# Decode attention over 64 heads: V of pair 30 in two halves, 64 stationary tokens in the last pair, and unused matmuls in the gaps of TensorE between its last parts

## The chip, the cores and the metric

The kernel runs on one core of a Trainium2 chip. The metric is device time in microseconds (us) of one execution, without the profiler's help; the profile of one execution is read beside it. Its span, from the first instruction to the last, is some 2 us shorter than the measured time (671.3 us for the run of 673.07 us that was profiled before). "Full" and "half" clock are the granted TensorE clock of 1.0 and 0.5 in the trace.

## The reference, cut to what matters

Two independent attention blocks, A and B, are computed for one query token each, with 32 heads, 8192 cached tokens and 128 channels per head; the two output rows of 512 are put side by side.

```python
q = (x @ wq)                                   # 1 x 32 heads x 128
scores = einsum("bhqd,bhkd->bhqk", q, k_cache) * 128 ** -0.5
p = softmax(scores)
o = einsum("bhqk,bhkd->bhqd", p, v_cache)
y = o.reshape(1, 32 * 128) @ wo                # ... A and B, concatenated
```

K and V of 64 heads in bf16 are 268 MB, read once. The kernel treats heads in pairs: 32 pairs, 0 to 31, each with one K and one V of 4 MB.

## The kernel before

K and V pass through a ring of five slots of 4 MB in SBUF. The order of the last transfers is K30, K31, wo (output weights of B, without its last two heads), V29, V30, V31 in three parts, the two heads of wo. For each pair, DVE multiplies K by q (`plan_M`, L422), TensorE folds the 128 products of a token to 8 with identity matmuls of 512 columns (`plan_fold`, L177 and L181, two halves a pair), DVE sums those (`plan_R`), a short exchange finds the maximum, ACT does exp, and TensorE multiplies with V:

```python
def plan_PV(j, t0=0, t1=TP, end=TP):                  # "wide": V moves, 512 columns a matmul,
    ...                                               # four matmuls side by side in the array
    for i in range(t0, t1, TB):                       # TB = 4 tokens x 128 partitions
        g = (i // TB) % CG
        m = e.matmul(ot_ps[...][32 * g:32 * g + 2 * TB, :], p2[:, ..., i:i + TB, :], t[:, i:i + TB, :], ...)
    ...                                               # then ACT copies ot_ps to o8
def plan_ot(j, last=True):                            # the fp32 "turn": 8 matmuls on o8, L552
    W('PE', c_cp, cp_val[j])                          # waits for that copy
    ...
def plan_PVturned(j, t0, t1):                         # "stationary tokens": V is the weight, 2 columns move
    for i in range(t0, t1):
        m = e.matmul(st_ps[1][:, 0:2], t[:, i, :], p2[:, ..., i, :], ...)
```

TensorE works in program order. Its last stage, for pairs 29 to 31, reads as follows (calls of other engines cut). `plan_y` multiplies 24 and then 4 finished heads with wo, 4 matmuls a head with one moving column each: the "light" stretch. `plan_ysq` is an output block of 8 matmuls for one pair.

```python
plan_PV(j - 2)                  # V29, 32 wide matmuls, L526: "the start of the last stage" below
plan_tr(j); plan_ot(j - 2); ...
for b in early: plan_y(LA, *b[:2])                    # 96 light matmuls, L652
plan_w_ready(j - 2); plan_sum(j); ...; plan_y(...)    # 16 more, L652
plan_PV(j - 1); plan_ot(j - 1); plan_o(j - 1)         # V30
LW = LAST_PARTS[NLW - 1][1]                           # parts (0, 64), (64, 96), (96, 128); NLW = 2
for i, (t0, t1) in enumerate(LAST_PARTS):             # V31
    W('PE', *part_of[i])                              # wait for this part's transfer
    if t1 <= LW:
        plan_PV(j, t0, t1, LW)
    else:
        if t0 == LW:
            plan_ot(j, False)                         # the turn stands BEHIND the wait
        plan_PVturned(j, t0, t1)                      # last 32 tokens
    if i == 0:
        plan_ysq(0)
plan_o(j)
plan_ysq(1)                                           # last output block, L689; DVE casts, SP stores
```

Of the kernel before, what the change touches and what calls it, by code (L numbers as in the profile page):

```python
# [39 lines left out]
def bass_concat_heads__mha_block_cached__gqa_block_cached__decode_kernel(  # L40
# [23 lines left out]
    Dh = ks[0].shape[3]  # L64
# [12 lines left out]
    NPR = NA * PPA  # L77
# [24 lines left out]
    with ExitStack() as st:  # L102
# [56 lines left out]
        def W(eng, ctr, val):  # L159
            if val is None or val <= 0:  # L160
                return
            if waited.get((eng, ctr.name), 0) >= val:
                return
            waited[(eng, ctr.name)] = val
            prog[eng].append((ctr, val))

        def OP(eng, fn):
            prog[eng].append(fn)
# [104 lines left out]
        land_of = {}  # L273
# [24 lines left out]
        assert order[-1] == ('v', NPR - 1)  # L298
        for name in order:
            item(name)  # L300
        LAST_PARTS = [(0, 64), (64, 96), (96, 128)]
        NLW = 2
        part_of = {}
        wo_early = wo_plan[LA][:-1]
        issued = [0]

        def dma(dst, src, ctr):
            v = ctr.bump(16)
            OP('SP', lambda e: e.dma_start(dst, src).then_inc(ctr.sem, 16))
            return v  # L310

        def issue(n):
            kind, idx = queue[n]
            s = n % NS
            if n >= NS:
                assert free_of[n - NS] is not None, (queue[n], queue[n - NS])
                for ctr, val in free_of[n - NS]:
                    W('SP', ctr, val)
            if kind in ('k', 'v'):
                a, jj = divmod(idx, PPA)  # L320
                t = (ks if kind == 'k' else vs)[a][0, 2 * jj:2 * jj + 2]
                src = t.rearrange("h (p t) d -> (h p) (t d)", t=TP)
                if (kind, idx) == ('v', NPR - 1):
                    for i, (t0, t1) in enumerate(LAST_PARTS):
                        part_of[i] = (s_part[i], dma(ring[:, s, t0 * Dh:t1 * Dh],
                                                     src[:, t0 * Dh:t1 * Dh], s_part[i]))
                else:
                    land_of[(kind, idx)] = dma(ring[:, s, :], src, s_slot[s])
            elif kind == 'wq':
                land_of[(kind, idx)] = dma(  # L330
                    ring[:, s, 0:NC_ * H * Dh],
                    wqs[idx].rearrange("(p c) n -> p (c n)", p=P), s_slot[s])
            else:
                for blk in wo_early if idx == LA else wo_plan[idx]:
                    land_of[('wo', idx, 0)] = (s_slot[s], load_wo(idx, s, blk, s_slot[s]))
            if (kind, idx) == ('v', NPR - 1):
                h0, n_, pm = wo_plan[LA][-1]
                for i in range(n_):
                    ctr = s_part[len(LAST_PARTS) + i]
                    land_of[('wo', LA, 1 + i)] = (ctr, load_wo(  # L340
                        LA, slot_of[('wo', LA)], (h0 + i, 1, pm), ctr))

# [71 lines left out]
        def kv(name):  # L414
            return ring[:, slot_of[name], :].rearrange("p (t d) -> p t d", d=Dh)
# [96 lines left out]

        def plan_PV(j, t0=0, t1=TP, end=TP):

            if ('v', j) in land_of:
                landed('PE', ('v', j))
            W('PE', c_e, e_val[j])
            W('PE', c_init, INIT)
            if t0 == 0 and j >= 1:
                W('PE', c_cp, cp_val[j - 1])  # L520
            t = kv(('v', j))

            def op(e):
                for i in range(t0, t1, TB):
                    g = (i // TB) % CG
                    m = e.matmul(ot_ps[j % NS % 2][32 * g:32 * g + 2 * TB, :],  # L526
                                 p2[:, j % NS, i:i + TB, :].rearrange("p t h -> p (t h)"),
                                 t[:, i:i + TB, :].rearrange("p t d -> p (t d)"),
                                 start=(i < TB * CG), stop=(i >= end - TB * CG))
                if t1 == end:  # L530
                    m.then_inc(c_pv.sem, 1)
            OP('PE', op)
            if t1 < end:
                return
            v = pv_val[j] = c_pv.bump()
            if end == TP:
                release(('v', j), (c_pv, v))
            W('ACT', c_pv, v)
            if j >= 1:
                W('ACT', c_ot, ot_val[j - 1])  # L540
            cp_val[j] = INC('ACT', c_cp, lambda e: e.copy(o8[:, j % NS % 2, :], ot_ps[j % NS % 2][:]))  # L541
# [16 lines left out]

        def plan_PVturned(j, t0, t1):
            t = kv(('v', j))  # L560

            def op(e):
                for i in range(t0, t1):
                    m = e.matmul(st_ps[1][:, 0:2], t[:, i, :], p2[:, j % NS, i, :],
                                 start=False, stop=(i == TP - 1), skip_group_check=True)
                if t1 == TP:
                    m.then_inc(c_ot.sem, 1)
            OP('PE', op)
            if t1 == TP:
                ot_val[j] = c_ot.bump()  # L570
                release(('v', j), (c_ot, ot_val[j]))
# [59 lines left out]
        def plan_y(a, h0, n):  # L631

            W('PE', *land_of[('wo', a, 0)])
            W('PE', c_w, w_val[(a, h0)])
            first = h0 == 0
            if first and a:
                W('PE', c_ye, a)
            last = not any(pm and b > h0 for b, _, pm in wo_plan[a])
            v = c_y.bump() if last else None

            def row(e):
                for i in range(n):
                    m = e.matmul(y_ps[0:1, :], w_bf[:, a, h0 + i:h0 + i + 1], wo_of(a)[:, h0 + i, :],  # L643
                                 start=(first and i == 0), stop=(last and i == n - 1),
                                 skip_group_check=True)
                if last:
                    m.then_inc(c_y.sem, 1)

            def cols(e):
                for i in range(n):  # L650
                    for b in range(NB):
                        m = e.matmul(y_ps[:, b:b + 1], wo_of(a)[:, h0 + i, b * P:(b + 1) * P],  # L652
                                     w_bf[:, a, h0 + i:h0 + i + 1],
                                     start=(first and i == 0 and b == 0),
                                     stop=(last and i == n - 1), skip_group_check=True)
                if last:
                    m.then_inc(c_y.sem, 1)
            OP('PE', cols if a == LA else row)
            if not last:
                return  # L660
            W('ACT', c_y, v)
            if a != LA:
                release(('wo', a), (c_y, v))
                ve = INC('ACT', c_ye, lambda e: e.copy(y_row[:], y_ps[0:1, :]))
                W('ACT', c_ye, ve)
                s_out.bump(16)
                OP('ACT', lambda e: e.dma_start(
                    out[0, 0:1, a * NOUT:(a + 1) * NOUT], y_row[:]).then_inc(s_out.sem, 16))
                return
            ve = INC('ACT', c_ye, lambda e: e.copy(y_bulk[:], y_ps[:, 0:NB]))  # L670
            W('PE', c_ye, ve)
            if qw_free[0]:
                W('PE', *qw_free[0])
            OP('PE', lambda e: e.matmul(qw_ps[0:NB, 0:P], y_bulk[:], ident_f[:],
                                        start=True, stop=False, skip_group_check=True))

        def plan_ysq(i):
# [18 lines left out]
            if last:  # L696
# [6 lines left out]
                    out[0, 0, LA * NOUT:(LA + 1) * NOUT].rearrange("(b m) -> b m", b=NB),  # L703
                    y_sb[:]).then_inc(s_out.sem, 16))



        for a in range(NA):
# [6 lines left out]
        def plan_w_ready(jo):  # L715

            for h0, n, pm in perm_l:
                if h0 not in w_done and LA * PPA + (h0 + n) // 2 - 1 <= jo:
                    w_done.add(h0)
                    plan_w(LA, h0, n)  # L720

        marks = []
        for j in range(NPR):
            marks.append({eng: len(ops) for eng, ops in prog.items()})
            c = j >= 1
# [50 lines left out]
        plan_o(j - 2)  # L776
        for b in early:
            plan_y(LA, *b[:2])
        plan_w_ready(j - 2)
        plan_sum(j)  # L780
        plan_ri(j)
        assert len(w_done) == len(perm_l) and len(direct_l) == 2
        for b in perm_l[len(early):]:
            plan_y(LA, *b[:2])
        plan_PV(j - 1)
        plan_ot(j - 1)
        plan_o(j - 1)
        LW = LAST_PARTS[NLW - 1][1]
        for i, (t0, t1) in enumerate(LAST_PARTS):
            W('PE', *part_of[i])  # L790
            if t1 <= LW:
                plan_PV(j, t0, t1, LW)
            else:
                if t0 == LW:
                    plan_ot(j, False)
                plan_PVturned(j, t0, t1)
            if i == 0:
                plan_ysq(0)
        plan_o(j)
        plan_ysq(1)  # L800
        assert issued[0] == len(queue)
# [82 lines left out]
```

## Time and profile before

| | before |
|---|---|
| time | 672.9 us, median of 3 (672.36 to 673.01); profiled run 673.07 us, span 671.3 us |
| traffic | 285 MB, mean 425 GB/s |
| last part of V31 landed | 665.58 us |
| from there to the last instruction's end | 5.7 us |
| last stage, from V29's matmuls (647.67) to the end of the cast (669.41) | 21.7 us, of which 2.1 us wait for V |

Two rows of the page, busy share in 40 equal slices, in tenths; the first is the granted clock of TensorE:

```profile
PEclk9998876779877767888876789877767888798787
DMA  9999999999999999999999999999999999999995
```

The DMA engines are busy until the last transfers run out (share 1.00 from 659.49 to 662.90 us, 0.46 in the 3.41 us after that). The chain of waits (start, duration in us, what) therefore ends in one long transfer and what follows it:

```profile
...
635.32 30.26 DMA ring<-in_B_v_cache_dram
665.58 0.04 issue
665.62 1.26 PE stps L552 x8
666.89 0.87 PE stps L564 x32
...
667.85 0.19 DVE sq L585
...
668.08 1.03 PE qwps L689 x8
...
669.13 0.28 DVE y_sb L699
```

The eight fp32 turns L552 do not need the last part of V; they wait for it by program order alone. The next fence is the timeline of TensorE in the last stage, with one line of ACT (start, duration, engine, line, count, and in brackets the idle time before it and what ended it):

```profile
...
647.67 1.90 PE L526 MATMUL otps<-ring,p 128*8 128x512 bf16 x32
...
655.99 3.80 PE L526 MATMUL otps<-ring,p 128*8 128x512 bf16 x29
660.47 1.05 PE L552 MATMUL stps<-sel,o 128*128 128x2 f32 x8 [0.68 <-ACT o L541]
661.45 1.04 PE L526 MATMUL otps<-ring,p 128*8 128x512 bf16 x16
662.31 0.61 PE L689 MATMUL qwps<-ring,sq 128*4 128x128 bf16 x8
663.13 0.60 PE L526 MATMUL otps<-ring,p 128*8 128x512 bf16 x8 [0.20 <-DMA ring<-in_B_v_cache_dram]
663.78 0.58 ACT L541 COPY o<-otps 128x512 f32<-128x512 f32 x1 [3.37 <-PE otps L526]
...
665.62 1.26 PE L552 MATMUL stps<-sel,o 128*128 128x2 f32 x8 [1.89 <-DMA ring<-in_B_v_cache_dram]
```

The bracketed 0.20 and 1.89 us are 2.1 us of waits for V. The turn also needs ACT's copy of the wide matmuls' sums, which ended at 664.36 us; where no transfer was late, a turn with nothing in between began 0.68 to 0.79 us after the wide matmuls before it. V29's 32 wide matmuls take 1.90 us and V30's take twice as long, because the clock differs. The windows between the clock's steps show it (stretch, length, busy us of each engine with counts, granted clock, DMA share, GB/s):

```profile
649.25:652.66 3.41, 2.92 (x63) 2.46 (x56) 0.44 (x2) 1.53 (x5) 0.00 (x0) 1.00 1.03 442
652.66:656.07 3.41, 3.11 (x86) 2.81 (x87) 0.52 (x3) 0.35 (x3) 0.00 (x0) 0.50 0.99 413
656.07:659.49 3.42, 3.42 (x33) 1.22 (x25) 0.00 (x0) 0.00 (x0) 0.00 (x0) 0.50 0.93 393
659.49:662.90 3.41, 2.73 (x37) 1.77 (x32) 0.18 (x1) 0.58 (x1) 0.00 (x0) 1.00 1.00 411
```

The clock fell after the first of these, though TensorE is shown busy for 2.92 of 3.41 us: from 650.26 us on, 2.4 us, that is matmuls with one or two moving columns (the turn, two small ones, and 1.1 us of the light stretch). It rose after the third window, which V30's matmuls filled.

"Activity" of a window, below, is my count from the trace: moving columns over the granted rate (about 2.4 columns a ns at full clock, as 15 folds of 512 columns took 3.24 us), a quarter for the wide matmuls that run four side by side, four times for fp32 (at half clock one of 128 columns, L674, took 0.42 us), over 3.41 us. These four windows have 0.08, 0.35, 0.92 and 0.38.

### The profile page before, as it was taken

Reading aid. Unit: us, or ns where it says so; the run is one execution under the profiler, and the core shown is the slowest. Engines: PE = TensorE matmul, PEld = TensorE weight load, DVE = VectorE, ACT = ScalarE, POOL = GpSimd, SP = SyncE. Lnnn points to the kernel's source line nnn. Section 1 sums busy time; section 2 is a strip of 40 time slices with the busy share of each in tenths; the row PEclk is TensorE's granted clock in tenths of the full one; section 3 lists DMA queues with packets and bytes.
Section 4 is the critical chain, followed back from the end, with each engine's and each line's share of the span. In section 5 each row is a group of like instructions: output and inputs, shape, how many; then the busy total and the mean of one; then the engine's idle time right before and its main releaser. Section 6 shows DMA issues by size and latency. Waiting matters only on the chain.

```text
span 671.3 us, 6004 instructions
## 1 busy us (share of the span) xinstructions
PE 439.0 (65%) x2782; PEld 102.8 (15%) x1822; DVE 387.5 (58%) x517; ACT 61.9 (9%) x203; POOL 2.4 (0%) x16
## 2 busy tenths in 40 slices
PE   2765775655677666567765655777566567757696
PEld 0200110101111010111111101111011111121134
DVE  5194566665555666555566665556666555555840
ACT  0101101001111001111100011110101111101010
POOL 1000000000000000000000000000000000000000
PEclk9998876779877767888876789877767888798787
DMA  9999999999999999999999999999999999999995
GB/s 375 437 437 433 430 421 431 437 436 432 421 428 437 437 433 430 420 435 437 433 435 428 424 435 437 433 433 422 430 437 435 433 428 424 433 436 429 426 422 240
DMA packets 10953, 285.38 MB, mean 425 GB/s; under 512 B 1211, under 2 KB 1726, under 8 KB 1854
## 3 DMA queue, kind: packets, MB, share of 16 engines
q1 hardware_dynamic: 10936, 285.22, 99.0%
q8 instruction: 8, 0.13, 0.1%
q14 instruction: 3, 0.02, 0.0%
q10 hardware_dynamic: 6, 0.00, 0.0%
HBM read 285.21 MB, written 0.00 MB: 425 GB/s over the span
## 4 chain that ended last, share of the span: by engine, by line
DMA 62%; PE 24%; DVE 11%; issue 2%; SPq 0%; DVEq 0%
DMA ring<-in_B_k_cache_dram 30%; DMA ring<-in_A_k_cache_dram 28%; PE fold L181 15%; DVE ring L422 8%; DMA ring<-in_B_v_cache_dram 5%; PE otps L526 3%; PE fold L177 2%; PE stps L552 1%; DVE s_sb L448 1%; PE yps L643 1%; DVE m L459 1%; PE stps L477 1%; DVE wt L614 0%; DVE w_bf L623 0%; DVE rinv L502 0%
## 5 line engine op out<-in xcount | busy, mean ns | idle before, releaser
L422 DVE TENSOR_TENSOR ring<-ring,qbc 128x2048 bf16<-128x2048 bf16 x256 | 298.4, 1216 | 166.5 <-DMA ring<-in_A_k_cache_dram 93.7
L181 PE MATMUL fold<-ring,ident 128*128 128x512 bf16 x960 | 276.3, 452 | 0.0
L467 PE MATMUL stps<-ident_f,m 128*2 128x128 f32 x32 | 11.1, 348 | 141.7 <-DVE rinv L502 140.2
L177 PE MATMUL fold<-ring,ident 128*128 128x512 bf16 x64 | 31.4, 491 | 64.6 <-DVE ring L422 64.6
L526 PE MATMUL otps<-ring,p 128*8 128x512 bf16 x1016 | 62.7, 387 | 0.2 <-DMA ring<-in_B_v_cache_dram 0.2
L552 PEld LDWEIGHTS stps<-sel,o 128*128 128x128 f32 x256 | 33.6, 192 | 157.3 <-issue 152.1
L448 DVE TENSOR_REDUCE s_sb<-fold 128x64 f32<-128x512 f32 x64 | 44.0, 688 | 3.2 <-PE fold L181 2.6
L483 ACT COPY nb<-stps 128x1 f32<-128x1 f32 x32 | 5.1, 159 | 419.2 <-PE stps L477 419.2
L585 DVE TENSOR_TENSOR ot<-stps,rinv 128x2 f32 (+1 forms) x30 | 4.8, 160 | 62.5 <-PE stps L552 62.5
L552 PE MATMUL stps<-sel,o 128*128 128x2 f32 x256 | 30.9, 243 | 3.1 <-DMA ring<-in_B_v_cache_dram 1.9
L541 ACT COPY o<-otps 128x512 f32<-128x512 f32 x32 | 18.7, 585 | 135.7 <-PE otps L526 135.7
L489 ACT ACTIVATE p<-s_sb,nb 64x128 bf16<-64x128 f32 x64 | 28.0, 437 | 3.8
L496 PEld LDWEIGHTS stps<-rowsum,ones_f 128*128 128x128 f32 x64 | 12.3, 194 | 98.7 <-issue 97.9
L467 PEld LDWEIGHTS stps<-ident_f,m 128*2 128x2 f32 x32 | 2.6, 81 | 158.8 <-DVE m L459 132.0
L526 PEld LDWEIGHTS otps<-ring,p 128*8 128x8 bf16 x1016 | 22.5, 87 | 24.3 <-issue 1.6
L387 PE MATMUL qwps<-ring,xsel 128*128 128x512 bf16 x64 | 18.6, 443 | 9.3 <-ACT qbc L394 4.8
L459 DVE TENSOR_REDUCE m<-s_sb 64x1 f32<-64x128 f32 x64 | 17.9, 280 | 2.1
L177 PEld LDWEIGHTS fold<-ring,ident 128*128 128x128 bf16 x64 | 6.4, 99 | 78.0 <-issue 59.6
L614 DVE TENSOR_TENSOR wt<-qwps,hmask 128x512 f32<-128x512 f32 (+3 forms) x5 | 2.2, 441 | 21.4 <-PE qwps L607 21.3
L477 PE MATMUL stps<-m,sel 2*128 2x1 f32 x64 | 12.1, 256 | 0.0
L489 ACT ACTIVATION_READ_ACCUMULATOR p<-s_sb,nb 64x1 f32 x64 | 11.6, 181 | 0.0
L477 PEld LDWEIGHTS stps<-m,sel 2*128 2x128 f32 x64 | 9.4, 182 | 10.5 <-issue 10.0
(49 smaller groups left out, 80.1 us busy)
## 6 DMA issues: line engine op xcount, KB each, us to landing
ring<-in_A_k_cache_dram SPq DMA_DIRECT2D x16, 4096.0 KB, 39.4
ring<-in_A_v_cache_dram SPq DMA_DIRECT2D x16, 4096.0 KB, 31.9
ring<-in_B_k_cache_dram SPq DMA_DIRECT2D x16, 4096.0 KB, 39.4
ring<-in_B_v_cache_dram SPq DMA_DIRECT2D x15, 4096.0 KB, 32.0
ring<-in_A_wq_dram SPq DMA_DIRECT2D x1, 4096.0 KB, 12.1
ring<-in_B_wq_dram SPq DMA_DIRECT2D x1, 4096.0 KB, 21.4
ring<-in_A_wo_dram SPq DMA_DIRECT2D x1, 4096.0 KB, 39.9
ring<-in_B_wo_dram SPq DMA_DIRECT2D x1, 2048.0 KB, 34.6
```

The source lines that it names most:

```text
L177: return e.matmul(out, lhsT, rhs, start=start, stop=stop)
L181: return e.add_instruction(mybir.InstMatmult(name=nc.get_next_instruction_name(), engine=e.engine, ins=[e.lower_ap(rhs), e.lower_ap(lhsT)] ...
L387: m = e.matmul(qw_ps[:, :].rearrange("p (j d) -> p j d", d=Dh), xsel[:, a, c, par, :], wq[:, c, 4 * g:4 * g + 4, par, :], start=(i == 0), ...
L422: m_val[(j, i)] = INC('DVE', c_m, lambda e: e.tensor_tensor(t, t, qbc[:, at(j, 1), :].broadcast_to([P, CH, Dh]), ALU.mult))
L448: r_val[(j, h)] = INC('DVE', c_r, lambda e: e.tensor_reduce(s_sb[:, j % NS, h * HT:(h + 1) * HT], fold_ps[h][:, :].rearrange("p (t e) -> p ...
L459: m1_val[j] = INC('DVE', c_m1, lambda e, h=h, q0=q0, q1=q1: e.tensor_reduce(m1[q0:q1, j % NS, h:h + 1], s_sb[q0:q1, j % NS, :], AX.X, ALU. ...
L467: tr_val[j] = INC('PE', c_tr, lambda e: e.transpose(st_ps[0][0:2, 0:P], m1[:, j % NS, :], ident_f[:]))
L477: bc_val[j] = INC('PE', c_bc, lambda e: e.matmul(st_ps[0][:, P:P + 1], sel2[:], m2[0:2, j % NS:j % NS + 1], start=True, stop=True))
L489: e_val[j] = INC('ACT', c_e, lambda e, h=h, q0=q0, q1=q1: e.activation(p2[q0:q1, j % NS, :, h], s_sb[q0:q1, j % NS, :], AF.Exp, bias=nb[q0 ...
L526: m = e.matmul(ot_ps[j % NS % 2][32 * g:32 * g + 2 * TB, :], p2[:, j % NS, i:i + TB, :].rearrange("p t h -> p (t h)"), t[:, i:i + TB, :].r ...
L541: cp_val[j] = INC('ACT', c_cp, lambda e: e.copy(o8[:, j % NS % 2, :], ot_ps[j % NS % 2][:]))
L552: m = e.matmul(st_ps[1][:, 0:2], o8[:, j % NS % 2, i * Dh:(i + 1) * Dh], sel8[:, 2 * i:2 * i + 2], start=(i == 0), stop=(last and i == TB ...
```

## The change

The intent: begin on V30 before all of it has landed; after the last landing have only 16 tokens left, with the turn already done; and keep the clock full with matmuls whose result nobody reads.

```diff
-        LAST_PARTS = [(0, 64), (64, 96), (96, 128)]
-        NLW = 2
+        LAST_PARTS = {NPR - 2: [(0, 64), (64, 128)],
+                      NPR - 1: [(0, 64), (64, 96), (96, 112), (112, 128)]}
+        NLW = 1
 ...   (each part is one transfer with its own semaphore, waited for in plan_PV and plan_PVturned)
+        def plan_fill(n):                      # n matmuls of 512 columns into a free PSUM bank
+            W('PE', c_r, r_val[(NPR - 1, 1)])
+            ...  e, fold_ps[0][:, :], ident[:], xsel[:, 0, 0:2]...., start=True, stop=True
 ...
         for b in early: plan_y(LA, *b[:2])
+        for t0, t1 in LAST_PARTS[j - 1][:-1]:
+            plan_PV(j - 1, t0, t1)
         plan_w_ready(j - 2) ...
-        plan_PV(j - 1)
+        plan_PV(j - 1, *LAST_PARTS[j - 1][-1])
         plan_ot(j - 1)
         plan_o(j - 1)
-        ...  (the loop over V31's parts shown above)
+        plan_ysq(0)
+        for t0, t1 in LAST_PARTS[j][:NLW]:
+            plan_PV(j, t0, t1, LAST_PARTS[j][NLW - 1][1])
+        plan_fill(3)
+        plan_ot(j, False)
+        for i, (t0, t1) in enumerate(LAST_PARTS[j][NLW:]):
+            plan_PVturned(j, t0, t1)
+            plan_fill([4, 2, 2][i])
         plan_o(j)
         plan_ysq(1)
```

More of the change, by code (lines that the diff above doesn't have):

```diff
@@ L300, in bass_concat_heads__mha_block_cached__gqa_block_cached__decode_kernel @@
             item(name)
-        LAST_PARTS = [(0, 64), (64, 96), (96, 128)]
-        NLW = 2
+        LAST_PARTS = {NPR - 2: [(0, 64), (64, 128)],
+                      NPR - 1: [(0, 64), (64, 96), (96, 112), (112, 128)]}
+        NLW = 1
         part_of = {}
+        next_part = [0]
         wo_early = wo_plan[LA][:-1]
@@ L322, in issue @@
                 src = t.rearrange("h (p t) d -> (h p) (t d)", t=TP)
-                if (kind, idx) == ('v', NPR - 1):
-                    for i, (t0, t1) in enumerate(LAST_PARTS):
-                        part_of[i] = (s_part[i], dma(ring[:, s, t0 * Dh:t1 * Dh],
-                                                     src[:, t0 * Dh:t1 * Dh], s_part[i]))
+                if kind == 'v' and idx in LAST_PARTS:
+                    for t0, t1 in LAST_PARTS[idx]:
+                        ctr = s_part[next_part[0]]
+                        next_part[0] += 1
+                        part_of[(idx, t0)] = (ctr, dma(ring[:, s, t0 * Dh:t1 * Dh],
+                                                       src[:, t0 * Dh:t1 * Dh], ctr))
                 else:
@@ L338, in issue @@
                 for i in range(n_):
-                    ctr = s_part[len(LAST_PARTS) + i]
+                    ctr = s_part[next_part[0] + i]
                     land_of[('wo', LA, 1 + i)] = (ctr, load_wo(
@@ L513, in plan_PV @@
         def plan_PV(j, t0=0, t1=TP, end=TP):
-            if ('v', j) in land_of:
+            if j in LAST_PARTS:
+                W('PE', *part_of[(j, t0)])
+            else:
                 landed('PE', ('v', j))
@@ L560, in plan_PVturned @@
             t = kv(('v', j))
+            W('PE', *part_of[(j, t0)])
             def op(e):
@@ L704, in plan_ysq, with op @@
                     y_sb[:]).then_inc(s_out.sem, 16))
+        def plan_fill(n):
+            W('PE', c_r, r_val[(NPR - 1, 1)])
+            def op(e):
+                for i in range(n):
+                    (held_matmul if i else matmul)(
+                        e, fold_ps[0][:, :], ident[:],
+                        xsel[:, 0, 0:2].rearrange("p c k m -> p (c k m)"), start=True, stop=True)
+            OP('PE', op)
         for a in range(NA):
@@ L784, in bass_concat_heads__mha_block_cached__gqa_block_cached__decode_kernel @@
             plan_y(LA, *b[:2])
-        plan_PV(j - 1)
+        plan_PV(j - 1, *LAST_PARTS[j - 1][-1])
         plan_ot(j - 1)
         plan_o(j - 1)
-        LW = LAST_PARTS[NLW - 1][1]
-        for i, (t0, t1) in enumerate(LAST_PARTS):
-            W('PE', *part_of[i])
-            if t1 <= LW:
-                plan_PV(j, t0, t1, LW)
-            else:
-                if t0 == LW:
-                    plan_ot(j, False)
-                plan_PVturned(j, t0, t1)
-            if i == 0:
-                plan_ysq(0)
+        plan_ysq(0)
[6 more added lines that the diff above has]
+            plan_fill([4, 2, 2][i])
         plan_o(j)
```

## The prediction

> **What bounds the kernel now.** Transfers. The page gives the DMA engines 0.9 or more in 39 of 40 slices, 285 MB at 425 GB/s, and the chain of waits ends with one DMA stretch of 30.26 us (635.32 to 665.58, V) and a compute tail. Only that tail, 5.7 of 671.3 us, can be shortened: 1.26 us the eight fp32 turns L552 (which wait for the last part of V only by program order), 0.87 us 32 stationary tokens L564, 0.19 us DVE L585, 1.03 us output matmuls L689, 0.28 us cast, then the store.
>
> **What the change intends.** After the last part landed: 16 tokens instead of 32 (0.44 us less), the fp32 turn moved in front of that wait (1.26 us less), and a warm clock for L689 (0.61 us at 662.3, 1.03 us at 668.1: 0.4 us less). If TensorE is always ready in time, that is about 2 us gained, less 0.15 us for two more DMAs (landings of V31: 4.90, 2.48, 2.50 us, 9.88 against 9.71 us for a whole V).
>
> **Why I doubt it.** TensorE has too little slack in the last 11 us. By the timeline V30 is whole at 655.7 us and TensorE begins on it at 655.75; there is no wait for the halves to fill. The first half merely runs earlier (from about 654.1), and the work that followed there (1.7 us from L607 to L674) moves behind it, so both halves again end near 659.6. Between there and the end before has slack only from 663.7 to 665.6. The change puts into it the turn (1.0), 32 more stationary tokens in place of 8 wide matmuls (0.4 more), and 3+4+2 unused matmuls of 512 columns (0.213 us each at full clock by L181, 0.43 at half: 1.9 to 3.9 us). It also stops hiding the wait for DVE before the first output block (0.4 us). Summed from traced durations, in order, at full clock, the last 16 tokens end near 668.1 us, 2 us after their data, against 667.75 before; the warm L689 gives 0.4 back: a tie.
>
> The clock can make it worse. The Trainium skill, "TensorE: Matmul & The Clock Gate", Part 1, states a free-running window of about 3.4 us and half clock as default; the trace agrees: the granted clock fell at 652.7, rose at 659.5, fell at 666.3, two windows apart. By my count of moving columns over this trace's windows, half clock ended only after windows at least 0.8 active (0.73 was not enough) and full clock fell at 0.25 or less (0.38 held). Before, the undivided V30 (32 matmuls in 3.9 us) is what filled window 656.1 to 659.5. Divided into 1.9 us pieces around light work, no window gets there (about 0.6), so ot, V31's 16 wide matmuls (0.86 to 1.9 us) and the fills run at half clock: 1 to 3 us later, by window phase.
>
> **Prediction.** Estimate from these terms: 0 to +3 us; mixed with the chance that I misjudge order or clock and the intended gain appears (-1 to -2 us): 673.8 us, 80% range 671.3 to 676.0. Faster by over 2%: 0.01, same 0.98, slower 0.01.
>
> **What would show it.** Right: granted clock 0.5 between 659.5 and 663 or later; fills followed directly by turned matmuls, without DMA waits; the chain of waits passing through TensorE from V30 on, its last DMA piece ending before 665. Wrong: a DMA wait just before the last 16 tokens and a tail of about 3.7 us after 665.7.
>
> **What would make it wrong.** A full clock from 656 on, V30's first half finding a gap earlier than I read, or another window phase in other runs.

## The result, and the profile after

| | before | after |
|---|---|---|
| time, median (range) | 672.69 us (672.36 to 673.01), 4 runs | 677.54 us (676.54 to 678.09), 4 runs |
| ratio of fast runs | | 1.0070, 95% interval 1.0053 to 1.0088 |
| span of the profiled run | 671.3 us | 675.1 us |
| last part of V31 landed | 665.58 us | 665.60 us |
| start of the last stage | 647.67 us | 649.39 us |
| from there to the end of the cast | 21.7 us | 24.1 us |

A ratio is the mean time of one kernel's fast runs over that of the other's of the same rounds, so not quite the ratio of the medians quoted. The time lies above the range of the prediction (671.3 to 676.0).

The transfers are not to blame: with two more of them the last part lands 0.02 us later (in the nineteen traces of this document it landed between 665.22 and 665.76 us). The chain of waits of the kernel after no longer contains them. Its last DMA piece ends at 568.5 us, with K of pair 28; from there on it runs through DVE and TensorE only, and ends:

```profile
...
659.59 1.96 PE otps L532 x13
...
661.57 0.59 ACT o L547
662.16 0.04 issue
662.21 1.88 PE stps L558 x8
...
665.43 1.71 PE otps L532 x13
667.13 0.33 issue
667.47 1.02 PE fold L181 x2
668.49 0.79 PE stps L558 x8
669.27 0.80 PE stps L571 x32
670.08 0.24 PE fold L177
670.31 0.65 PE fold L181 x3
670.96 0.38 PE stps L571 x16
...
671.80 0.38 PE stps L571 x16
```

The last 16 tokens landed at 665.60 us and TensorE comes to them at 671.80, more than 6 us late. The unused matmuls (fold, here L177 and L181 on data of the kernel's start) follow the other work and are followed by it, with no wait for a transfer anywhere: the only gaps that they fill are those behind ACT's copy (0.7 us) and DVE's product (0.3 us). The windows of this trace:

```profile
651.25:654.67 3.42, 2.93 (x71) 2.71 (x68) 0.44 (x2) 1.73 (x6) 0.00 (x0) 1.00 1.00 426
654.67:658.08 3.41, 3.41 (x69) 1.97 (x65) 0.14 (x1) 0.00 (x0) 0.00 (x0) 0.50 1.01 420
658.08:661.49 3.41, 3.11 (x36) 1.34 (x35) 0.38 (x3) 0.16 (x1) 0.00 (x0) 0.50 0.98 407
661.49:664.91 3.42, 2.38 (x17) 2.28 (x17) 0.18 (x1) 0.58 (x1) 0.00 (x0) 0.50 0.88 340
664.91:668.32 3.41, 3.08 (x23) 1.29 (x21) 0.00 (x0) 0.58 (x1) 0.00 (x0) 0.50 0.08 28
```

The clock is at half from 654.67 to 668.32 us, four windows; before it was at half for two. My activity of these four is 0.52, 0.75, 0.17 and 0.84. From TensorE's timeline, V29 and the two halves of V30:

```profile
...
649.39 1.90 PE L532 MATMUL otps<-ring,p 128*8 128x512 bf16 x32
...
655.83 1.88 PE L532 MATMUL otps<-ring,p 128*8 128x512 bf16 x16
...
659.60 1.91 PE L532 MATMUL otps<-ring,p 128*8 128x512 bf16 x13
...
```

Where the 4.1 us of later cast (669.41 to 673.48) come from:

- 1.7 us stood there before the first changed instruction: the last stage started at 649.39 instead of 647.67 us.
- Up to the end of V30 the two are equal, 12.1 us from that start in both traces (659.79 and 661.51). Dividing V30 gave nothing here, as TensorE had no wait to fill.
- From V30's end to the cast's end before takes 9.6 us, of which 1.4 are slack (0.20, and 1.2 of the 1.89 us, as the turn also needs ACT's copy: TensorE could come about 1.4 us later before anything ended later), so 8.2 of work and of waits for ACT and DVE; after takes 12.0 of these. The 3.8 more, from the two traces: about 2.1 of unused matmuls that no copy hides, 1.0 for V31's 16 wide matmuls at half clock, 0.8 for the turn of pair 30 (1.88 instead of 1.05), 0.8 for 32 more stationary tokens, 0.6 for the output block of pair 30 at half clock and its wait for DVE; less about 1.6 for 8 wide matmuls that went, and a faster last turn and last output block.

The 1.4 us of slack are used up, the rest, 2.4 us, is added to the 1.7.

### The profile page after: what moved, and what is told of

It is laid out like the page before. It is cut to its first block, busy times and chain, and to the rows that moved or that the text cites. A ratio compares the mean times of both kernels' runs of the same rounds, so it can differ in the third digit from the quotient of the medians.

```text
span 675.1 us, 6066 instructions
## 1 busy us (share of the span) xinstructions
PE 444.5 (66%) x2815; PEld 104.2 (15%) x1850; DVE 387.5 (57%) x517; ACT 61.9 (9%) x203; POOL 2.4 (0%) x16
## 4 chain that ended last, share of the span: by engine, by line
DMA 57%; PE 29%; DVE 11%; issue 2%; ACT 0%; SPq 0%; DVEq 0%
DMA ring<-in_B_k_cache_dram 29%; DMA ring<-in_A_k_cache_dram 28%; PE fold L181 18%; DVE ring L426 8%; PE otps L532 4%; PE fold L177 2%; PE stps L558 2%; DVE s_sb L452 1%; DVE m L463 1%; PE yps L650 1%; PE stps L481 1%; PE yps L659 0%; DVE wt L621 0%; DVE w_bf L630 0%; DVE rinv L506 0%
## 5 line engine op out<-in xcount | busy, mean ns | idle before, releaser
L181 PE MATMUL fold<-ring,ident 128*128 128x512 bf16 x960 | 279.7, 456 | 0.0
L177 PE MATMUL fold<-ring,ident 128*128 128x512 bf16 x64 | 31.4, 491 | 65.4 <-DVE ring L426 65.4
L532 PEld LDWEIGHTS otps<-ring,p 128*8 128x8 bf16 x1008 | 22.5, 87 | 23.4 <-issue 1.6
L391 PE MATMUL qwps<-ring,xsel 128*128 128x512 bf16 x64 | 16.9, 411 | 9.4 <-ACT qbc L398 4.8
L177 PEld LDWEIGHTS fold<-ring,ident 128*128 128x128 bf16 x64 | 6.4, 100 | 80.0 <-issue 61.3
L481 PE MATMUL stps<-m,sel 2*128 2x1 f32 x64 | 12.1, 256 | 0.0
## 6 DMA issues: line engine op xcount, KB each, us to landing
ring<-in_A_wq_dram SPq DMA_DIRECT2D x1, 4096.0 KB, 12.1
```

The costliest lines, as they stand in the source:

```text
L177: return e.matmul(out, lhsT, rhs, start=start, stop=stop)
L181: return e.add_instruction(mybir.InstMatmult(name=nc.get_next_instruction_name(), engine=e.engine, ins=[e.lower_ap(rhs), e.lower_ap(lhsT)] ...
L391: m = e.matmul(qw_ps[:, :].rearrange("p (j d) -> p j d", d=Dh), xsel[:, a, c, par, :], wq[:, c, 4 * g:4 * g + 4, par, :], start=(i == 0), ...
L481: bc_val[j] = INC('PE', c_bc, lambda e: e.matmul(st_ps[0][:, P:P + 1], sel2[:], m2[0:2, j % NS:j % NS + 1], start=True, stop=True))
L532: m = e.matmul(ot_ps[j % NS % 2][32 * g:32 * g + 2 * TB, :], p2[:, j % NS, i:i + TB, :].rearrange("p t h -> p (t h)"), t[:, i:i + TB, :].r ...
```

## The experiments

All kernels gave correct results. Runs of e1 to e9 and of "after again" were on one chip, where before ran 672.24 to 675.74 us; e9b to e12, e13 to e15 and e16 to e17 on three others. Times vary more on these four chips than in the runs of the result above, and the last stage of before and after starts anew in every run at another time; so means within 0.3% of each other are not told apart, and the traces have to help. The theory after reading the traces: TensorE is the one that ends the kernel after; it is late because the change gives it more work than it had slack, and the divided V30 leaves it at half clock for that work ("clock theory"). The rivals: the unused matmuls themselves are the loss at any clock; the order of the tail is; or the added transfers (already refuted by the landing above).

### One part of the change taken away, or one alone

**e1: V30 whole.** `LAST_PARTS` without the entry of pair `NPR - 2`, and one `plan_PV(j - 1)` where the second half stood:

```diff
-        LAST_PARTS = {NPR - 2: [(0, 64), (64, 128)],
-                      NPR - 1: [(0, 64), (64, 96), (96, 112), (112, 128)]}
+        LAST_PARTS = {NPR - 1: [(0, 64), (64, 96), (96, 112), (112, 128)]}
-        for t0, t1 in LAST_PARTS[j - 1][:-1]:
-            plan_PV(j - 1, t0, t1)
-        plan_PV(j - 1, *LAST_PARTS[j - 1][-1])
+        plan_PV(j - 1)
```

> The kernel after, with V of pair 30 loaded and used in one piece. Clock theory (the divided V30 keeps every clock window under the activity that lifts half clock): the 32 adjacent matmuls fill a window again, the clock is full from about 660 to 663 on, the fp32 turn of pair 30 takes 1.0 us instead of 1.86, the 16 wide matmuls of V31 0.9 instead of 1.9: about 674 to 675 us, 2.5 to 3.5 us faster than after. Rival (the 11 unused matmuls are the loss, in any clock): not over 0.5 us faster than after, 677 us.

Measured: 676.44 us (674.69 to 677.82), ratio to before 1.0041. The profiled run is the fastest, 674.69. In its trace the clock rose after the window that V30 filled (activity 0.78), and what follows ran at full clock:

```profile
...
657.16 3.62 PE L531 MATMUL otps<-ring,p 128*8 128x512 bf16 x29
661.49 1.05 PE L557 MATMUL stps<-sel,o 128*128 128x2 f32 x8 [0.70 <-ACT o L546]
...
```

From the start of the last stage to the cast it took 21.5 us instead of 24.1. The mechanism is as expected; the gain on after was less: 1.0 us of the medians (after again, below) or 1.5 by the ratios, where 2.5 to 3.5 were expected.

**e2: without unused matmuls.** The two calls of `plan_fill` go.

```diff
-        plan_fill(3)
-            plan_fill([4, 2, 2][i])
```

> The kernel after without its 11 unused matmuls. Rival (they are the loss): the 9 that stand before the last 16 tokens took about 2.5 us in the trace, so 675 us or below. Clock theory: the clock stays at half longer without them, the turn of pair 31 goes from 0.95 to 1.9 us and the last output matmuls from 0.6 to 1.0, so only about 1 us of it comes back: 676 to 676.5 us, and the granted clock at 0.5 from about 655 to the end.

Measured: 675.62 us (674.78 to 677.97), ratio 1.0029. The clock was at half from 653.6 us to the end and the turn of pair 31 took 1.86 us, as the clock theory said; but the times lie between the two expectations (1.8 us below after again; 1 was the clock theory's, 2.5 the rival's). The unused matmuls cost more than I gave them.

**e3: halves alone.** The loop of before for V31 (parts to 64, 96, 128, two of them wide, no fills; the edit is shown against before), V30 as in after.

```diff
+        LAST_PARTS = {NPR - 2: [(0, 64), (64, 128)],
+                      NPR - 1: [(0, 64), (64, 96), (96, 128)]}
 ...
+        for t0, t1 in LAST_PARTS[j - 1][:-1]:
+            plan_PV(j - 1, t0, t1)
 ...
-        plan_PV(j - 1)
+        plan_PV(j - 1, *LAST_PARTS[j - 1][-1])
```

> The kernel before, with V of pair 30 in two halves and nothing else changed. Clock theory: half clock from about 653 to the end; turn of pair 30 +0.85, wide matmuls of V31 +1.5, first output block +0.3, less the 1.9 us of slack before the last part: 673.5 to 675 us. Rival (fills): same as before within 0.3 us, 672.7 us, as only one DMA more is issued.

Measured: 674.37 us (673.09 to 676.91), ratio 0.9997: a miss for the clock theory as I had put it. The profiled run, 676.91, is the slowest; its last stage started at 651.3 us, ran at half clock from 655.4 to 669.1 and took 22.3 us. With a start at before's 647.67 the same stage would end at 669.9 us, 0.5 us behind before's; that the halves alone mostly vanish in the slack is my reading of this and of the mean, and no run of e3 that started early was traced.

**e4: V30 whole and no fills.** Both edits of e1 and e2.

> The kernel after with V30 whole and without unused matmuls: what is left is 64 stationary tokens, the turn ahead of the wait, the last part in two, and the first output block ahead of V31. Clock theory: TensorE is back in time for the last parts or within 1 us: 671.5 to 673 us, about as before or a little faster. If instead the new order of the tail itself (64 tokens, output block first) were the loss: 675 us or more.

Measured: 673.46 us (672.89 to 676.85), ratio 1.0006. So the order of the tail and its 64 tokens are not, alone, the loss. In its trace the clock fell again at 663.1 us.

**After again**, unchanged, beside the same runs of before.

> The kernel after once more, beside runs of before on the same chip as the next three: about 4 us slower than before, and the 32 matmuls on V of pair 29 (start of TensorE's last stage) anywhere between 647.5 and 651.5 us, as in the first six traces; from that start to the cast of the output about 24 us.

Measured: 677.45 us (675.47 to 680.29), ratio 1.0063; start 648.13 us, 24.0 us from there. With after at 1.0063, the four means form a square: taking the fills away gives 1.0063 to 1.0029 with halves and 1.0041 to 1.0006 without, 0.34% or 2.3 us both times; making V30 whole gives 1.0063 to 1.0041 and 1.0029 to 1.0006, 0.22% or 1.5 us both times. As best estimates the two add up, with 0.4 us left. But each step is no larger than the half width of its interval (e4: 0.9970 to 1.0042), so that either of them is not zero is not shown by these means alone.

**e5: halves loaded apart, used together.** Both `plan_PV` calls of V30 stand after the light work; transfers and fills as in after.

```diff
-        for t0, t1 in LAST_PARTS[j - 1][:-1]:
-            plan_PV(j - 1, t0, t1)
 ...
-        plan_PV(j - 1, *LAST_PARTS[j - 1][-1])
+        for t0, t1 in LAST_PARTS[j - 1]:
+            plan_PV(j - 1, t0, t1)
```

> The kernel after, V of pair 30 still loaded in two halves but both used together, after the light work. Clock theory: the 32 wide matmuls stand side by side again and lift the clock, so from the start of the last stage to the output's cast it takes 21.5 us as with V30 whole (24.1 in after), time as e1, 1 to 2 us below after. Rival (the second transfer costs it): 24 us, as after.

Measured: 676.33 us (673.89 to 678.78), ratio 1.0034 (0.9994 to 1.0074), by the ratios 2 us and by the medians 1.1 us below after. The trace shows what the place of use does: with the halves side by side the clock rose at 659.8. But it fell again at 663.2, after a window of activity 0.38, all 11 fills then ran at half clock, and the stage took 24.9 us, which is a miss. In e1 windows of 0.38 and 0.39 held. The tail sits on the edge.

### The state in which TensorE enters its last stage

The last stage started, in the nine traces whose code before it is the same (before, after, after again, e1 to e6), at 647.7, 647.8, 647.9, 648.1, 648.3, 648.5, 648.9, 649.4 and 651.3 us. The kernel before gave the earliest. The first folds of pairs 28 to 31 take 3.6 us at full clock and up to 6.4 when they begin at half. Where the clock's windows lie differs by execution (the fall ahead of pair 29 came at 601.46 us in before, at 603.47 in after). The record gives the mean granted clock of untraced runs too, and for before it goes with the time: of its 37 runs on these chips the 22 under 674 us had 0.810 to 0.816, the five over 675.5 us 0.806 to 0.809.

**e6: the turn ahead of the wait**, in the kernel before.

```diff
         for i, (t0, t1) in enumerate(LAST_PARTS):
+            if t0 == LW:
+                plan_ot(j, False)
             W('PE', *part_of[i])
 ...
-                if t0 == LW:
-                    plan_ot(j, False)
```

> The kernel before, only with the fp32 turn of pair 31 put ahead of the wait for the last part of V. If the last landing ends the chain: 1.2 us faster than before in runs whose last stage starts before about 648.5 us; in late runs, where TensorE ends the chain, nothing. About 0.7 us faster in the mean. The output matmuls stay at half clock (1.0 us).

Measured: 673.06 us (671.59 to 676.0), ratio 0.9999, interval 0.9964 to 1.0034: the mean shows nothing. The trace (671.59 us, start 648.29) shows what was meant: the turn ran at 664.58, the 32 tokens followed at 665.50 with their data in place since 665.38, the stage took 19.6 us and the cast ended at 667.9 instead of 669.4. That a late start takes it away in the slower runs is not shown, as they were not traced (the one of 676.0 us had a mean clock of 0.806, the one of 674.0 us 0.813, hardly below the traced run's 0.814).

**e9: fills before the folds**, in the kernel before: 6 after V, 4 ahead of the first fold, for pairs 29 to 31, where TensorE waits for DVE.

```diff
+            if j > LE:
+                plan_fill(4, (j - 1, 0))
             plan_fold(j, 0)
 ...
                 plan_w_ready(j - 2)
+                plan_fill(6, (j, 0))
```

> The kernel before, with unused matmuls where TensorE really waits: 6 after V and 4 before the first fold of pairs 29, 30 and 31. Clock theory: the first folds there take 3.4 us instead of 5 to 6, the last stage starts at 647 us or earlier in every run, and the times gather at 672.3 to 672.8 us without the late runs of 674 to 676 that before has on this chip. If the late start has another cause than the clock: spread and median as before, or slower by the fills.

Measured: 673.62 us (672.77 to 674.24), ratio 0.9996. The spread is smaller (before on this chip, with more runs: 672.24 to 675.74), the mean did not move. Two windows still had 0.15 and 0.24 activity, and two of three first folds still began at half clock; start 647.15. Inconclusive by itself: too few fills.

**e9b: more of them**, 12 (5 in the last gap) and 7.

> The kernel before with 12 (5 in the last gap) and 7 unused matmuls ahead of the first folds of pairs 29, 30 and 31, in place of 6 and 4, which left windows of 0.15 and 0.24 active and let the clock fall. Clock theory: the clock stays full from 577 to about 652 us, the first folds take 3.4 to 3.6 us, the 32 matmuls on V of pair 29 start at about 645.5 us (647.15 with fewer, 647.7 in before) and no run is over 673.5 us. If the late start is not the clock's: start at 647 or later and runs up to 675.

Measured: 673.95 us (673.07 to 674.47), ratio 0.9999. The clock stayed full from 578.5 to 650.1 us, every first fold of pairs 29 to 31 took 3.6 us and the stage started at 645.87: half of the expectation. But no run was below the median of before (672.77 in these rounds):

```profile
...
645.87 1.90 PE L526 MATMUL otps<-ring,p 128*8 128x512 bf16 x32 [1.77 <-DMA ring<-in_B_v_cache_dram]
...
655.58 3.58 PE L526 MATMUL otps<-ring,p 128*8 128x512 bf16 x32 [1.14 <-DMA ring<-in_B_v_cache_dram]
659.86 1.86 PE L552 MATMUL stps<-sel,o 128*128 128x2 f32 x8 [0.69 <-ACT o L541]
...
```

TensorE, now early, waits for V29 and V30. Waits make the windows emptier still: this time the clock went to half at 650.1 and stayed there to the end, so the last stage took 24.5 us. Being early is of use only with the clock held.

**e10: e9b, the turn ahead of the wait, and the last 32 tokens in two transfers** (edits of e9b and e6, and `LAST_PARTS = [(0, 64), (64, 96), (96, 112), (112, 128)]`).

> The same fills ahead of the folds, the turn of pair 31 ahead of the wait for the last part of V, and the last 32 tokens in two transfers of 16. Both theories of a gain from a TensorE that is on time: it waits for the last 16 tokens, which land near 665.6; cast near 667.9 instead of 669.4: 671 us, 1.5 us below the fast runs of before, and in every run.

Measured: 672.43 us (671.66 to 674.04), ratio 0.9989, not told from before. The cast ended at 668.1 in the trace (671.66 us); the slower runs have no trace.

**e11: after with e9b's fills.**

> The kernel after, whole, with these fills ahead of the folds. If after is slow because TensorE enters its last stage too late for what the change adds there: start 645.5 instead of 648 to 649.4, end earlier by as much, 673.5 to 675 us, 3 us below after, though its own last stage still takes about 24 us. If the fills inside the tail are the loss: 677 as before.

Measured: 673.17 us (672.66 to 678.37), ratio 0.9992. Four of five runs took 672.7 to 673.5 us, as before in the same rounds (median 672.77), though no part of the change was taken back. The profiled one took 678.37: its clock fell at 655.1 and stayed at half to the end (window activities 0.67, 0.29, 0.75, 0.27, 0.61), and its last stage took 27.4 us. This is one kernel with two outcomes 5 us apart. The four fast runs have a mean granted clock of 0.824 to 0.827, the slow one 0.813; that the phase of the windows alone parts them is my inference, as they were not traced.

**e12: e1's tail with its output block behind V31, 6 fills in the tail, and e9b's fills.**

```diff
-        plan_ysq(0)
         for t0, t1 in LAST_PARTS[j][:NLW]:
             plan_PV(j, t0, t1, LAST_PARTS[j][NLW - 1][1])
-        plan_fill(3)
+        plan_ysq(0)
+        plan_fill(1)
         plan_ot(j, False)
 ...
-            plan_fill([4, 2, 2][i])
+            plan_fill([2, 1, 2][i])
```

> The tail of after with V30 whole, the first output block behind V31's wide matmuls, 6 instead of 11 unused matmuls there, and the fills ahead of the folds. If TensorE is on time and warm: the last 16 tokens wait for their data at 665.6, the output matmuls take 0.6: cast near 667.4, 670.5 to 671 us. If the clock falls in the tail: 672 to 673.

Measured: 673.24 us (671.13 to 676.43), ratio 1.0009: one profiled run as good as hoped (the last tokens did wait for their data, cast 667.8), others not.

### The clock held

From V29 to V30 the light stretch lets the clock fall in every trace so far. The next kernels put 2 unused matmuls behind every 4 heads of it, and 2 each ahead of the turn of pair 29, ahead of the light matmuls and after `plan_sum`:

```diff
                     for b in range(NB):
                         m = e.matmul(y_ps[:, b:b + 1], wo_of(a)[:, h0 + i, b * P:(b + 1) * P], ...)
+                    if i % 4 == 3 and i < n - 1 + (not last):
+                        for f in range(2):
+                            (held_matmul if f else matmul)(e, fold_ps[0][:, :], ident[:], ...)
```

**e13: e12 with these.**

> The kernel e12 (tail of after with V30 whole, output block behind V31, fills ahead of the folds) with 2 unused matmuls after every 4 heads of the light output matmuls and 2 at three more places there. Clock theory: clock full from 577 us to the end in every phase, V30's 32 wide matmuls 1.9 us instead of 3.6, cast near 667.5 to 668 us, 671 to 671.8 us in all runs, none over 673 (e12 ran 671.1 to 676.4). Rival (the tail's order is the loss): still runs of 674 and more.

Measured: 671.0 us (670.67 to 671.67), ratio 0.9970, interval 0.9952 to 0.9988. All five runs lie below the fastest of before (672.2 in these rounds). In the trace the clock was full from 606.7 us to the end of the work (it was at half from 603.3, against the expectation). V30's wide matmuls take 1.9 us, and the chain of waits ends in the transfer again, without a turn behind it:

```profile
...
633.49 32.27 DMA ring<-in_B_v_cache_dram
665.76 0.05 issue
665.81 0.55 PE stps L570 x16
666.36 0.24 PE fold L177
666.60 0.22 PE fold L181
666.81 0.55 PE qwps L701 x8
...
```

**e14: e11, so the whole change, with these.**

> The kernel after, halves and 11 fills included, with the fills ahead of the folds and in the light stretch. Clock theory: the last stage takes about 23 us instead of 24 to 27 though it holds 16 more unused matmuls, the fp32 turns 1.05 us, cast near 669 us, about 672.5 us, none over 674. If halves and order cost by themselves: 674 to 677 at full clock too.

Measured: 673.7 us (673.28 to 677.05), ratio 1.0028. Better than after (1.0070 and 1.0063, on other chips), but a miss: slower than expected, and two of six runs near 677. In the trace (673.36 us) the clock was full through the whole stage, the turns took 1.05 us, and TensorE still ended the chain, reaching its last tokens at 668.24, 2.9 us after they had landed at 665.36:

```profile
...
665.72 0.80 PE stps L571 x32
...
668.24 0.38 PE stps L571 x16
...
669.07 0.55 PE qwps L702 x8
...
```

So the change's work has a price at full clock too: the rival holds a part.

**e15: e10 with these.**

> The kernel e10 (before, with fills ahead of the folds, the turn ahead of the last wait, the last 32 tokens in two transfers) with the same matmuls in the light stretch. Clock theory: cast near 667.8 us, 671.3 to 672 us in all runs (e10: 671.7 to 674.0), 1.0 to 1.5 us below the median of before. If the added matmuls make TensorE late: 672.5 or more.

Measured: 670.96 us (670.71 to 671.85), ratio 0.9968, interval 0.9951 to 0.9986. The clock did fall at 664.4 in its trace, which is of the slowest of the five runs, 671.85 us. It differs from before in eight places of the diff, uses no halves and no stationary tokens beyond before's 32, and with e13 is the best version found: 1.9 us below the median of before. Before with the added matmuls alone, without either new tail, was not run, so how much of this gain is theirs is not shown.

**e16: e13 with V30 in halves again**; **e17: e14 with V30 whole**, so the change's order and its 11 tail fills alone, at held clock.

> e13 (clock held at full) with V of pair 30 in two halves again. Theory (the halves cost only through the clock): at full clock they are 0.9 us each and nothing else moves, so within 0.3 us of e13: 671.0 to 671.4 us. Rival (the halves cost by order or transfer): 672 or more.

> e14 with V30 whole: clock held at full, the output block first and 11 unused matmuls between the last parts. Theory: 9 matmuls of 0.215 us (1.9 us) and 0.4 us of waiting for DVE stand before the last 16 tokens, and only part of it meets a wait for data: cast 1.5 to 2.3 us behind e13's, 672.5 to 673.5 us. Rival (the halves were e14's loss): 671.3.

Measured: e16 671.88 us (670.89 to 672.38), ratio 0.9969, against 0.9970 of e13: with these matmuls the halves cost nothing that the runs can tell. Even so the clock was not held throughout: in e16's trace it was at half from 660.25 to 663.66 us, after a window of activity 0.38. e17 672.57 us (671.78 to 673.74), ratio 0.9986: 0.16% or 1.1 us above e13, less than the means can tell apart. The traces point the same way (cast 668.52 against 667.67 us, 0.85 us), so the order with the 11 fills seems to have a price of its own, less than expected. e14 stands a further 0.42% above e17. Between the two traced runs the difference lies ahead of the stage: e14's clock fell at 589.7 and again at 606.8 us, the first folds of pair 29 took 4.5 us instead of e17's 3.6, and its stage began at 647.21 instead of 646.03; from there e14 took 22.7 and e17 22.5 us, both at full clock. Why two runs of e14 took 677 us is open: their mean granted clock, 0.825, is that of its fast runs (0.822 to 0.830), so a lost clock is not what the record shows.

### The edge, over all traces

In the traces of the sixteen kernels e1 to e17 and those of before, after and after again, from 570 us to the windows that end by 666 us, 142 windows ran at half clock and 372 at full. Sorted by my activity count they split almost cleanly: of those at half clock, 75 of at most 0.76 were followed by half again and 67 of at least 0.75 by full; of those at full clock, 58 of at most 0.38 were followed by half and 314 of at least 0.31 kept it. The decisive window of the kernel after (658.08 to 661.49, which holds the second half of V30) had 0.75 and stayed at half; "after again" 0.76 and e2 0.76, the same; with V30's matmuls together e1 had 0.78, e4 0.80 and e5 0.82, and rose. Dividing V30 takes just enough away, but by the last hundredth my count decides nothing: e12 with V30 whole and e16 with it in halves had 0.75, and rose.

## Why the prediction was wrong

Right in it, step by step:

- The bound and the tail were read correctly, and the halves found no wait to fill: V30 ends 12.1 us after the start of the last stage in both traces.
- The clock stayed at half where it said (0.5 "between 659.5 and 663 or later": to 668.3), for the reason given, the divided V30. This was close to luck: it put that window at "about 0.6" and the edge at 0.8; the window had 0.75, and the edge over all traces is at 0.75 to 0.76.
- The fills are "followed directly by turned matmuls, without DMA waits", and the chain of waits leaves the transfers.
- The nine unused matmuls before the last tokens took about 2.7 us, inside its "1.9 to 3.9 us".

Wrong, and by size:

- The step that failed is the sum, "Estimate from these terms: 0 to +3 us", and in it a term that was taken as fixed: the time at which TensorE enters its last stage. It came from the one trace at hand, 647.7 us, the earliest of nine (the middle one is 648.3, the latest 651.3). In the traced run of after the stage began at 649.39, and 1.7 of the 4.1 us by which the cast is late stood there already. Before swallows about 1.4 us of such lateness in its waits for V. After has no waits left, and every bit of it counts. With a start at 648.13 (after again) the cast came 2.7 us after before's, inside the sum, and the run took 675.47 us. Measured were +4.9 us, +4.3 by the ratio on the second chip; that late starts make up the untraced runs too is not shown.
- The terms of the tail were sized well. From V30's end to the end of the last tokens the sum has 8.5 us at full clock (659.6 to 668.1); e14 took 8.2 at full clock (660.44 to 668.62). At half clock after took 10.6 (661.55 to 672.17), 2.4 more, inside "1 to 3 us later".
- The slack "from 663.7 to 665.6" is 1.9 us in its text; 0.7 of it was the copy for which the turn has to wait anyway.
- Mixing in "the chance that I misjudge order or clock and the intended gain appears" took a further 0.5 us or so off the middle of the sum (+1.5 to about +1.0). No run of after showed that gain; the fastest of eight took 675.47 us.
- The "0.15 us for two more DMAs" were not seen: the last part landed 0.02 us later.
- "A tie" at full clock fits e14's trace (673.36 us, before's 673.07) but not its mean of 1.0028.

What stays open: the share of after's runs with a whole tail at half clock, as one run of each kernel is traced (two of after), and the two slow runs of e14.

## What to carry to other kernels

Work added to an engine "in its gaps" is free only if the gaps are there in the order in which the engine runs: list what it waits for, at which times, and subtract; here there were about 1.4 us, as part of each wait for data hides another wait, and the change asked for 3.8. Where the clock depends on recent activity, one trace shows one phase of it: look at several runs before a sum of single microseconds, and put unused matmuls where the engine does the lightest work, ahead of the critical stretch, not into it. Held that way, the same ideas gave kernels 0.3% faster than before in the mean, with every run below the fastest of before (e13, e15).

## What the Trainium skill lacked or had wrong

- "TensorE: Matmul & The Clock Gate", Part 1: The HAM clock gate, gives the window (3413 ns, free-running) and the two states; this case agrees (steps 3.41 us or multiples apart, clock 1.0 or 0.5 only). It says that one busy window raises the clock and one idle window lowers it, but not how busy. By my count of a window's moving columns the runs put the rise at 0.75 to 0.76 and the fall between 0.31 and 0.38; between these both outcomes occur.
- The same page, "HAM oscillation", warns of gaps of TensorE. Here the clock fell without a gap over 0.5 us: TensorE was shown busy for 2.92 of 3.41 us, 2.4 us of it with matmuls of one or two moving columns, activity 0.08. I found no page that says how little such matmuls count.
- The same page, "LDWEIGHTS", gives a load's time by its columns without the clock. Eight fp32 turns (128 columns of weights, 2 moving) took 1.05 us at full and 1.86 at half clock; 32 bf16 loads of 128 columns with 2 moving took 0.94 and 0.99. So one follows the clock and the other hardly does.
- Part 1 advises not to fit a model to a specific count of slow matmuls at the start, as the penalty is worth under 1% of a typical kernel's span. The size of the differences here agrees (e11: 672.7 to 678.4 us, 0.9%, if the clock is what parts its runs), but that is as large as the effect under study, and with the clock held the spread was smaller (e13: 670.7 to 671.7 us).
- "DMA: Bandwidth & Descriptors", "Anatomy of one DMA", gives some 2 us of fixed cost for one transfer, for the path through GpSimd; this kernel issues from SP. I found no page that says what one more costs in a queue that is never empty: two more, of 16 and 4 KB a partition, moved the last landing by 0.02 us, less than it differs between traces (665.22 to 665.76 us).
